# The largest |K| taken over blocks as they lie, then over 128 turned tokens, with a newly searched instruction order

## The chip, the cores and the metric

The kernel runs on one core of a Trainium2 chip. A core has five engines with a queue each: TensorE (PE; its weight loads are listed as PEld), VectorE (DVE), ScalarE (ACT), GpSimd (POOL) and SyncE (SP). TensorE writes its results to PSUM, here eight banks of 128 x 512 float32; VectorE and ScalarE read them there. The metric is the device time of one execution in microseconds (us).

## The reference

Two layers read inputs of 2048 tokens by 640 channels; their outputs stand side by side.

Part A is a gated long convolution. `k` is convolved with a filter of four taps and multiplied by `v`; the product `kv` is convolved over all 2048 tokens with a filter of its own per channel (by FFT in the reference), `kv * ssm_D` is added, and the sum is multiplied by `q`.

```python
y = irfft2(rfft2(kv_pad) * rfft2(kf_pad))[:, :S]
y = y + kv * ssm_D[None, None, :]
return q * y
```

Part B is attention with a memory: 32 heads of 20 channels, four segments of 512 tokens.

```python
logits = einsum('bhqd,bhkd->bhqk', qs, ks) * scale + mask
p = softmax(logits); a_dot = einsum('bhqk,bhkd->bhqd', p, vs)
pq = phi(qs); num = einsum('bhld,bhde->bhle', pq, M); den = einsum('bhld,bhd->bhl', pq, z) + 1e-06
o = g * (num / den) + (1.0 - g) * a_dot
M = M + einsum('bhld,bhle->bhde', phi(ks), vs); z = z + phi(ks).sum(l)
```

The heads are joined again and multiplied by `wo`.

## The kernel before

**The program is recorded, then issued in a stored order.** `Layer` calls `conv` for five blocks of 128 channels (`dp` 0 to 4) and `project` and `attend` for eight units `u` (segment `u // 2`, half `u % 2` of the heads), with `load_x` and `project_out` once a segment. None of these calls issues anything: a `Recorder` notes each instruction, or each run of matmuls under `rec.one()`, as an operation with its predecessors, and `price` (line 190) gives it a duration for an offline search. The result of that search stands in the file as two packed texts: `ORDER`, the place of every operation, and `BASE`, the first PSUM bank of every group of results. `issue` unpacks them and emits the operations in that order, so each engine's queue is the part of `ORDER` that belongs to it, and an instruction waits for those ahead of it on its engine and for the data it needs. All instructions have the line of `issue`, 253, in the profile; they are told apart by the tiles they write and read.

**Part A, per block.** `load_filter` brings 128 channels of `ssm_k` (tiles `ET` or `kT`) and turns them so that tokens lie on partitions: block 0 by TensorE matmuls with the identity `ident`, the others by a VectorE copy and a DMA transpose. `short_filter` applies the four taps (`kr`, `skd`) and multiplies by `vt`. `spectrum` multiplies by the DFT table `Wf`, copies eight PSUM results with ScalarE into `F` (one buffer, `FBUF = 1`, shared by both kinds and all blocks) and adds and subtracts on VectorE into `Xh` or `Kh` (keys `BX`, `BK`); in the first group of a filter's spectrum a matmul with weights `ones` adds `ssm_D` out of `Drow`, a 128 x 640 tile whose first row alone is not zero (line 459). `product` multiplies the spectra on VectorE (`pq`, `Y`), `inverse` goes back with `Wi`, multiplies by `q` (`outa`), and POOL's queue stores.

**Part B, per unit.** `project` (line 569) multiplies 128-token tiles of `xT` with `wqkv`. ScalarE copies K and Q into `KQ` (128 tokens, four tiles, K or Q, 16 heads, 32 places of which 20 are channels and the 21st of K is 1), and V into `Va`. SyncE's queue turns each tile by DMA into `KQT`, where head and channel lie on partitions and the tokens along them. `phi` makes `PP`, which is turned to `PqT`.

Softmax takes no row maximum. In its place a bound is subtracted inside the score's matmul: for each head and channel the largest |K| over the 512 tokens, `kam`, is taken on VectorE out of `KQT` (lines 607 and 608); `A` spreads it over the heads with a sign; |Q| (`qabs`, an AND with 0x7fff on `KQT`) is multiplied by `A` on TensorE; ScalarE copies the result to `bT`; and four small DMAs on SyncE's queue write its rows into `KQT`'s Q beside the ones of K. Every score of the unit needs them.

`attend` makes the scores block by block (A below the diagonal, D on it with the mask from `mleft` and `mright`, J for two joined), ScalarE takes the exponential of 128 x 1024 at a time into `ET` (seven buffers), TensorE multiplies by `Va` and adds the memory's part (`PqT`, `Mbd`), and VectorE divides (`rr`, `o`, `o_s`). `project_out` turns `o_s` and multiplies by `wo`.

**Constants.** POOL clears `Drow`, `ones`, the unused places of `KQ` and `PP`, and loads the small tables; SyncE and ScalarE load the weights.

Of the kernel before, what the change touches and what calls it, by code (L numbers as in the profile page):

```python
# [774 lines left out]
ORDER = r"""
c-jrrgLW7S5Cy>9yLan0we8flZKt+v+qP{dwQbwBZR@>nm~$qrq!5vG5?#_uJc%qRC6#25jFMUcC9_PI88TBKCNU8~;z~pb5S6b&2``x>jpUL@5?>NX42dbRB(@}!#FA7JNiwM<NhG<XMHO+0h1`-&
(jkjfm8=p?vP%LaL=MR*$&mtCkQLeRT`Ef=e3QgThB%TEv5^XCP)G_(5h*GKq@a|N(vnB=N(m_`#iY38ll)Rf%1U}<KxU*yAmShilA^Z6M;$3AHKmqRlOU-saS;z0kqI@Vu{4o}(pnlxC@C)$rGnI#
Hqu<`$~<W)4Wy~mlk8|Ap(Tv8k^&fjoM<LJkpsEV3%PL<c~B5-rJW2!d+8vZWE_U0qm0K0OhZ0&k<OAAQ6#F2L{}+<Q5cJ<7=*#-jXvlm6EF-DF&(2Z2K_Mwvt_R2M_H6dIdqr8=pnN(1HEJjW@0G5
qc7^A9~!`I5<=Nz{6G;D!v}oC94U%V_>2e^(duKCL^m_qLM%d0`H3I$3;z(#!dnzuEK6ke|Af7zugt*$%*8@kB&ARqWw2D1$$VKL^AT3mqFNsrD#N6oR6s>6MkTD2Xf_Y9^%BEY$p%?28)b!Tl7?uE
{!$zz@l!U-02wHQqy}oD7HXpoN+71Kl}4zHDu`uOQ4LKHgu1AXb+Sd8Vz@Lzh^&zjvRZ<rIliDR+MzvKpcVe2CB9*Z43@3Z0Y@dQZIkWN5u>CvcF0aSD7z%G?Unr!PTF9kbjBe$ES<1Vy5P8U#cnwu  # L780
-OwF><d+<gV{%eX$ZzR^J#t#A>sOqTB{(Bz<(x#a0Q-$UI4>9El7zM}wg&6a(pp(3>uj+tuB}BE>uPbVkzJI=*3Oz+Z|h@&t%3ElB$m`#STAd618lrZka!l~5?gyqXvwUDtwu*1XrpC}jFSX5S*Az`
f^iUsa9OU%dL**3vH?`rNixWW*kNphsOkz#lT}!Wzw%Fp8nm`9#WI-I)8sbHuF7&um20vCJFyG9F;Vs)j7HF~8c}b^b-5`~HJXOfy$G$hB%I!s=o(&QXk?9~QM8T*XkFch$8rFhuo+vh72EJcj$l6;
>QOY(V>pGTdKzc39p`WyZLPmGvpaGgXK(@CteM`Ei?}O~<RtpqLpgyAmeG3HWn95kTtj#3XRR%hwXy4HVwZ3O59GeY)LUq32{o3cwRD!=5^Hizp^3D<p0NhnSd-{&G|`vxN?yxOeIs!+jV9ID8du|K
GQESlNMR{$q&<~q@?2g>DtnA4c!)=MinN+iQ)y}q)O0%BnrnK^Y+3Cd?&AUC>j=wY88oB*vrL*<v+5`tZDVb`J+&<Q%!FfXoTauj)=~qlmA26D_QN`AC;e*QEHrCsHp^}~ET`qQT-ILmS$^xFd-RRH
wU3tDYG^Ipss*f|6|th0#|qg;`6OTDt-O<BmQ4#=cKsl2wVig>E}B4#TMjK@IrTN(;In+P+?q@CXjko~`Lv|9);9XtUfFB=W4raQm9=tK-ty}+yq6bviMM!%=Xh+Ttc;bmC-w>xtb$dxDpu91S&&sU
r}3RtvYJNLvf5V1s#{&FVfE~#g<^fnt6@0NK3G^zvI6?s!n2@8WCRw{!usCYuq~h43!7roY^qgZRerI#Hs6|Zo+-g*Y{&L&&K8_ywYW>?*iWm?aGY*+INN60UM-^g^p{0qHO{cbw!|h|ab0T5te6(n
07heEF1HmHg>@OkMqFSG`5q;-q%N}38kGyJjF#2zy53gVY74dy+hCh)jjgouT29y6M%!$MwTJf99d<;kXeq6#TdbG%)}6M?`sh{*((Sg*_Ui%d#%g*{cUw(1<{{l@`|W@ow7z=CqI0P3wLNy!y6~8_
W&<|iaa(7H?Su`}&K#^m^rQ{cL3+ea*+?CwUD=(dtrO2$3=Y>G9HFCijP}>DI!*`ZHjT&ljLDX4#ql~pdvT&xXAMr$$vQ>ru|E5-1NSolPwR2*&Fy+ZPwFYn&NEs;r|D6xs8e;i&d?k@t2x<EXX-4S
t#fsb9@F!7!Om+(UeL>WMX%X)J7?$gqFu7fcE#rDRl8w*8JqnWhjDp>H`$Z@dDCuLWxdAh9KetK#DpBgL`=;4+@TNnlmod`Z`&QaYxnHFC1Fxl(qz1-cNvTKcuAk|8B;MelQShB*h70{?-|H6Ov`jk
!4F)fulSmInUDFIff<>J3p6vcFg@pMR=(g%F4D!iL>KCJUe#+_fCX8I*Y$?p(!wmtBFx1+ys7uKxaVeBmScH7)(R}f;(VyzSb`P#KufX|pXeif%o6^NPxY?e(`<aMFSIo8=rb+prTn$N(L#QQh5ajQ  # L790
`E%Cx;Vi>S9Kj#_$&sw$w^-F*>MQ-lKfKM~9Lw<>$K|?0SLsR}%)cDPe>AWBf5k)iR!4I=#o_PtgO1@^U8mDHoijL-Ls{N8=xv?F6<o<-Ea$WNUO(!3oxn+4t)CgJA^J%x_(Xo;WKLlNujEr%**EGY
{j5v4S-0q1F6BJV=K?O|GS1;5e$lV`P1oou26HtFctH<g4PV2xe8aa~$Fg42H*ym<a|^d}F}HC8ziVh;&oExyf9MYG<SrKTu)dpn7|tX3cJAd*-N$-f+RJ!-Kfv%F*$=XzH}YTVAfk9wZ|X%nq6c^#
uj`S#sMAAvV}Hm;tmZ-Pp2U-S6F<VE{H+x|nn(8-9@AraGmq`byt%jX*51-nd7!8ExE{~r`yWl<Ej*zo_mm#T6Zv0F>?e7O$9aP3J%wlT%$~)wdN$AQIXr`B^faE<5AiU&`acz<^PHZ`b9)}o>-jvt
clS2l&5zL#3ZVhC^>#keNBL;K%qzS|#c5t*d+*@k5FQcG(K~r(@8UhYr$<CoL_>7MKyUBkeZ8Oe_W?f8m-`qGgO%RP2l-$h;zNCy5BC*5!pHhJAMa;4!6*7zUgad8?B}@5&oeBhcqB~q=|00}`YfOA
0hr@+eV$+T>psor`vPC+i+r)K@m0Rg*ZUG*>#O~gAN9z%;lUo_SNyau^@D!MkNFng>YIGCpYtd<?-#huxBCX)=!gBdpYS7o#xM9uzv;L9s_*cNzSH;kHNWj={gUtXeZI?g`+h&*{{i6J>gE
"""
# [76 lines left out]
```

## Time and profile before

| | |
|---|---|
| median of 3 runs | 290.04 us (289.86 to 291.36) |
| the profiled execution | 290.99 us, its span 289.2 us |
| TensorE's mean granted clock in it | 0.987 of full speed |
| VectorE busy | 262.0 us, 398 instructions |
| ScalarE busy | 254.0 us, 391 instructions |
| TensorE busy (matmuls; weight loads) | 258.5 us; 195.3 us, 4226 each |
| exponentials into `ET` | 155.9 us, 160 instructions |
| `kam` reductions on VectorE | 18.2 us, 8 instructions |

The span runs from the first instruction to the last; the execution's own time has 1.8 us more around it. Busy time is the time in which an engine's instructions run, counted once where they overlap. Matmuls are pipelined and their ends are modelled, so TensorE's busy time also holds time in which it could take more. Where a row gives an idle time, the name behind it is what ended it. Rows of the timeline give the start, the duration, the engine, the operation, what it writes and reads, and how many instructions were merged.

### The profile page before, as it was taken

To read this page: it belongs to the slowest core of one execution; us is meant where nothing else is said; L and a number is where in the kernel's file an instruction comes from. 1 tells how busy PE (TensorE), PEld (TensorE's weight loads), DVE (VectorE), ACT (ScalarE), POOL (GpSimd) and SP (SyncE) were. 2 spreads that over 40 slices of the span, in tenths; PEclk is the share of its full clock that TensorE was granted. 3 is DMA by queue.
4 is the path that set the end of the run, shared out by engine and by line. 5 is a ranking of instruction groups with operands and counts; after the bars stand their busy time and mean duration, and the time that the engine had idled before them with its cause. 6 is when DMAs were issued, how large, how long until landed. Compare 5 with 4: busy or idle time off the path is not lost. (4 is left out here: it accounts for less than half of the span.)

```text
span 289.2 us, 9883 instructions
## 1 busy us (share of the span) xinstructions
PE 258.5 (89%) x4226; PEld 195.3 (68%) x4226; DVE 262.0 (91%) x398; ACT 254.0 (88%) x391; POOL 42.5 (15%) x71
## 2 busy tenths in 40 slices
PE   0999998789989899999989999998799977888895
PEld 0788756668667678777656888656586755656673
DVE  0569999999999999999999999999999999989554
ACT  1694899899998978999999999999979999989972
POOL 8300000001005000403100310022001220001620
PEclk9999999999999989999999999999799999999999
DMA  6999889899943779916696149952492029921252
GB/s 190 383 243 178 217 160 174 207 215 164 223 118 85 165 99 204 205 61 120 166 167 144 43 59 174 191 133 71 88 156 57 24 55 141 207 26 48 58 123 91
DMA packets 113500, 40.71 MB, mean 141 GB/s; under 512 B 105696, under 2 KB 111376, under 8 KB 113328
## 3 DMA queue, kind: packets, MB, share of 16 engines
q1 hardware_dynamic: 108624, 34.07, 61.8%
q0 software_dynamic: 2064, 4.76, 5.5%
q10 hardware_dynamic: 2768, 1.24, 1.8%
q8 instruction: 33, 0.54, 0.8%
q14 instruction: 11, 0.09, 0.1%
HBM read 14.11 MB, written 5.24 MB: 67 GB/s over the span
## 5 line engine op out<-in xcount | busy, mean ns | idle before, releaser
L253 ACT ACTIVATE ET<-ps 128x1024 bf16<-128x1024 f32 x160 | 155.9, 1064 | 6.7 <-PE ps L253 6.4
L253 PEld LDWEIGHTS <-xT 128*128 128x128 bf16 x640 | 60.5, 99 | 32.2 <-issue 10.8
L253 PE MATMUL ps<-wqkv,xT 128*128 128x320 bf16 x480 | 75.5, 303 | 3.6 <-ACT ET L253 1.9
L253 ACT CAST F<-ps 128x512 bf16<-128x512 f32 x80 | 43.0, 614 | 4.2 <-DVE F L253 1.6
L253 POOL DMA_DIRECT2D out_dram<-outa x32 | 22.2, 815 | 165.1 <-DVE outa L253 141.1
L253 PEld LDWEIGHTS <-ET 128*128 128x128 bf16 x1296 | 40.3, 97 | 4.1 <-issue 2.2
L253 PE MATMUL ps<-Va,ET 128*128 128x21 bf16 x1280 | 41.2, 172 | 0.1
L253 PE MATMUL ps<-KQT 32*128 32x128 bf16 (+2 forms) x896 | 34.5, 242 | 2.0 <-ACT ET L253 1.0
L253 PEld LDWEIGHTS <-Wf 128*128 128x128 bf16 x320 | 29.9, 98 | 6.5 <-issue 2.4
L253 ACT CAST KQ<-ps 128x320 bf16<-128x320 f32 x64 | 27.5, 454 | 3.7 <-PE ps L253 3.1
L253 PE MATMUL ps<-wo,xT 128*128 128x320 bf16 x160 | 25.2, 299 | 1.1 <-ACT ET L253 0.6
L253 PEld LDWEIGHTS <-KQT 32*128 32x128 bf16 x896 | 16.5, 94 | 12.0 <-issue 10.8
L253 PE MATMUL ps<-skd,kr 128*128 128x128 bf16 (+3 forms) x140 | 20.9, 301 | 1.1 <-ACT ET L253 1.0
L253 PE MATMUL ps<-Y,Wi 128*128 128x256 bf16 x160 | 20.3, 273 | 1.7 <-ACT ET L253 1.0
L253 PE MATMUL ps<-vt,Wf 128*128 128x256 bf16 x160 | 20.1, 272 | 1.8 <-DVE vt L253 1.4
L253 PE MATMUL ps<-kT,Wf 128*128 128x256 bf16 x160 | 21.2, 276 | 0.0
L253 PEld LDWEIGHTS <-kr 128*128 128x128 bf16 x140 | 17.3, 146 | 5.5 <-issue 2.7
L253 DVE TENSOR_TENSOR o<-ps,rr 128x640 bf16<-128x640 f32 x24 | 19.7, 823 | 0.7
L253 PE MATMUL ps<-mright,mleft 32*128 32x128 bf16 x512 | 14.4, 219 | 6.5 <-ACT ET L253 3.4
L253 PE MATMUL ps<-Mbd,PqT 128*128 128x84 bf16 x96 | 18.2, 202 | 1.9 <-ACT ET L253 0.9
L253 DVE TENSOR_TENSOR Y<-Y,pq 128x2048 bf16<-128x2048 bf16 (+1 forms) x20 | 18.6, 949 | 0.1
L253 DVE TENSOR_TENSOR pq<-Xh,Kh 128x2048 bf16<-128x2048 bf16 x15 | 18.3, 1223 | 0.4
(77 smaller groups left out, 356.4 us busy)
## 6 DMA issues: line engine op xcount, KB each, us to landing
vt<-in_A_v_dram SPq DMA_DIRECT2D x10, 256.0 KB
pq<-in_A_q_dram SPq DMA_DIRECT2D x10, 256.0 KB
out_dram<-outa POOLq DMA_DIRECT2D x32, 64.0 KB, 2.5
out_dram<-outb POOLq DMA_DIRECT2D x12, 160.0 KB, 3.1
ET<-in_A_ssm_k_dram SPq DMA_DIRECT2D x3, 512.0 KB
Wf<-c_wf SPq DMA_DIRECT2D x2, 512.0 KB
Wi<-c_wi SPq DMA_DIRECT2D x1, 1024.0 KB
kT<-in_A_ssm_k_dram SPq DMA_DIRECT2D x2, 512.0 KB
```

What stands on the lines that cost most here:

```text
L253: f(*[fix(a) for a in args], **{k: fix(v) for k, v in kw.items()})
```

## The change

Three things change.

1. **The maximum.** Once a unit's four tiles of K lie in `KQ`, VectorE clears the sign bits of all 4 x 16 x 20 values (into the `qabs` buffer), takes the maximum of tiles 0 and 1 against 2 and 3, and of the two that are left, into a new tile `kmax`, 128 tokens by 16 heads by 32 places (places 20 to 31 are cleared once by POOL). Four matmuls with the identity turn `kmax`, 128 columns for four heads, into one PSUM bank, and `kam` is reduced out of that bank, 512 elements where it was 2048. The rest of the bound is as before.
2. **The D term.** `Drow` is 128 x 128 now, with the five blocks of `ssm_D` in its first five rows; the weights are column `dp` of the identity, repeated 128 times, instead of `ones`, which goes.
3. **The order.** `ORDER` and `BASE` are new: the search took a DMA transpose to last at least 1260 ns (line 205), and charged stretches in which TensorE has few columns to do. `order` and `base` differ throughout, on every queue. No line of code shows the charge.

```diff
@@ price
-                op.dur = 5.1 * size / 1024
+                op.dur = max(1260, 5.1 * size / 1024)
@@ Layer.__init__
-        self.Drow = c.tile([128, D], bf16, name="Drow")
-        self.ones = c.tile([128, 128], bf16, name="ones")
+
+        self.Drow = c.tile([128, 128], bf16, name="Drow")
+        self.kmax = c.tile([128, 16, 32], bf16, name="kmax")
         rec.key = ("zero",)
         nc.gpsimd.memset(self.Drow[:], 0.0)
-        nc.gpsimd.memset(self.ones[:], 1.0)
+        nc.gpsimd.memset(self.kmax[:, :, DH:32], 0.0)
         rec.key = ("load", "Drow")
-        nc.gpsimd.dma_start(out=self.Drow[0:1, :], in_=self.ssm_D[None, :])
+        nc.gpsimd.dma_start(out=self.Drow[0:5, :], in_=self.ssm_D.rearrange("(c d) -> c d", d=128))
@@ spectrum
                                 if last and h == 0:
-                                    nc.tensor.matmul(o[:, 0:128], lhsT=self.ones[:], rhs=self.Drow[:, dsl], start=False, stop=False, grp=g, skip_group_check=True)
+                                    nc.tensor.matmul(o[:, 0:128], lhsT=self.ident[:, dp:dp + 1].to_broadcast([128, 128]), rhs=self.Drow[:], start=False, stop=False, grp=g, skip_group_check=True)
@@ project
+        rec.key = ("kmax", u)
+        ka = self.ring("qabs", [128, 4, L])[:].rearrange("p g q -> p (g q)")[:, 0:1280].rearrange("p (t h d) -> p t h d", t=4, h=16)
+        V.tensor_scalar(out=ka.bitcast(i16), in0=KQ[:, :, 0, :, 0:DH].bitcast(i16), scalar1=0x7fff, scalar2=None, op0=ALU.bitwise_and)
+        V.tensor_tensor(out=ka[:, 0:2], in0=ka[:, 0:2], in1=ka[:, 2:4], op=ALU.max)
+        V.tensor_tensor(out=self.kmax[:, :, 0:DH], in0=ka[:, 0], in1=ka[:, 1], op=ALU.max)
+        g = self.group(1, "kmax")
+        with rec.one():
+            for k in range(4):
+                nc.tensor.matmul(g.ap[:, 0, 128 * k:128 * k + 128], lhsT=self.kmax[:, 4 * k:4 * k + 4, :], rhs=self.ident[:], start=True, stop=True, grp=g)
         rec.key = ("bound", u)
         kam = self.ring("kam", [128, 4], f32, n=2)
-        V.tensor_reduce(out=kam[:], in_=KQT[:, 0], axis=AX.X, op=ALU.max, apply_absolute_value=True)
+        V.tensor_reduce(out=kam[:], in_=g.ap[:, 0, :].rearrange("p (k t) -> p k t", k=4), axis=AX.X, op=ALU.max, grp=g)
@@ ORDER and BASE
...
```

More of the change, by code (lines that the diff above doesn't have):

```diff
@@ L775 @@
 ORDER = r"""
[L776 to L795, printed above, removed]
+c-jrrgMttW5Czb=cV=>JwrjI(+um&3wry{=YqM?Jwr#$5KH{X33=&z=N(6~6BB>=%(n&;#C+Q`#q>z;IRboj-fqa*5qCzoABMBtFM3o#8P2xy^#E^tCT`EZ;sUle<k|dU-l0=eATuCOmB)nu2mu!+%
@@ new lines @@
+vP)X#lypqMgpA2p%q__o$gIr5s*;V_nS(hQTcXGei7AyO1yeE+(=#zMu#gm%0#Z<lNpT4!u{l%Xu#}XR5>is~Nq))2+$<tRB@dG^kK~myQdZ(JBQr4#Ye;RWBk>p{)ug6Wm&~jsNmyQzG8N;qoTTPl
+sVEhsp)``bY%EQrzBHG*(m=vUJqazXrH!<dR`QTVSd_(BoGqlOG?TW{PWrMR^D#dQax}-VgS3~9GKrHpkcBveV>w3(a2zMHlMLff&f;)(l_?y>L7d6)tjNkN%&DBg{v5#0GMHUtwgk&8na1gyz}XCD
+C3X|)2#(|&c9$M9m%U^mdrAqGq$pIi6r*Z*jiAvqy2j8S5>X>*IhN-y{^mS})(V`@6<o<5{K@#bfQz`8%h+4`$`Z!WFxrTXxs(fJp{(K(2`ft_tj5(o(uBjL3afIFES74VCrvqDnlqjz&}Qr>bvRVQ
+>2lWPPpQZHY`}!tUk1oPStiS+G|RFK6YECVB<p0otdNzmN><AT36X|OqSaZ0L9EGI+$>upkq(j;Y{l9fEW>4ljFOfdB5P!=v}PN2WG8m!NNLN}+$&pUn{;7Uw&M;-s!_B91GGK&$##jYf7p#XWtZ%i
@@ new lines @@
+e>@-u<&bn|5B6j){$+1Q)=-*EcS~~pEq(Y)4$BewBQZ6W2I?L;E+^!u9Fx;>QqIUJIV<O+t9H}#V(QvP+v-pqrv0?PUXY8DLbq@m$IArS%68gbd+BHyBPq4FUXn?YO8aOy*~m1SPB(KC`)XR9EK}sN
+q}I+_16_2irq?l=L5J%A9iantyiSvGIzj)+Kgp=uxq}mRvQ8DlL~%^fOgdF}l2DxFX`Z5BJwrHFfZB+T7}&ro5)R>UfDsT8kr4$^5e@ZlRj$cF9^zph;SCulYq*Y+^eETzy4;jd2#rVxKp2F@ZK;D@
++|4~a#=1Dp6Wq&vyd_U$KO3SE&hQ)`%UNFHWj4iCUgI4(&raG?hv;?QU^Cp6n;fZE*j+F1Hb?6{xy6gjqj~iX@A9GC;~>qa_c=-%<Gu{m2YkdHnh-fPw?2{w5)-jd9}VzQUP)r)($_LglcIx8*Cx25
+Ne~B5<(VWxY{bQ5#zQi6)XbV3Sv8BkkyLobK%~KQdCe4f&Nobrba)|Y@q{VylrNYbGjyiT(%CvkYa$5oQ41N65ij|QZ@Cj4kzWhyTX`pYP(bHuu>R4%`c*R{6S5#HzG*g9`ygA9L$hlbqa{Fqg|f)j
@@ new lines @@
+94$~t3u_TAs>QUVhPBXETsz^tl+u<kYlYHUM$2jmEvFUqqkNJtk{#KQ136J%V_7a#(u!JHt7uitjXcPQul&Z({KD^i$M>wJA6P>_@)N6TUi{ME`dNasmWH#M8qwM!l6}^8sIB$1zBbT?`bDEz3~Qu6
+wXU|te66GNw5c}J<{H6ZZjH5tw$wIgqS39D#<cL3AF-{q{!_69S{%g?$KqN%Td46Zfpta~bVWBT)+PE~+aroC)gRgcQ7wseu#UD11yB&Zt&i=-8eOMrwYjyhgqFyPpePdCARBCj(bIa_N?oM`Y@n^y
+LTG30t);cHWx8CuqX$-KQcGqjExGN*KBTbq8fY7JlWx{-wnew<BHgANG(@{v36w->?AHT2%C>76ltoYM(4D$Vck3SAs|U3g`rwcr#t|IR-Z-o$bf2EoDmbdCtS`!=6#C(mRz)=&*JC=|_TvD~X?Gi8
+BkjDN)?s#5FX%-bZI^V6^|#B~*M_654aOP0s@L?o-q3M20$pqf`q@AX!WA8FH+6!I#u$vmL>q-$Iu_$F$;x3UhT*oRw!7LNlWhRDA){ro@knExth3$IDc0KB*bvKXL#?!xwFx+gL%42ZZ4xG8GRoK#
@@ new lines @@
+Oton?!)Dqnn{E|Q5tT6&(~#DtqleAFLw%&_EWN$f4E9F1<226TI8LAvPT~}1;ykKj2VUxBywWSUuMcz<W@8Q>YcQ5zE-nC0&u%&Ft%mWOwiIFggMIuzKJ#!M-oM)q%VJqAo8_`Rb{0o*41X=J<+J=&
+zzSM!`(yv?nHI8lb`H<=y%n*dR?Lc93A>0(sA!d~k`=a+_D<jHS9_vQ^_x|(YF6E9SXFz85Bfqs>L)E{zb(khTLqhsd02$SSb&ANifah)8@P^}_+q8(7Ve^fHMB-{4~^|Hp5Q(n;1z0GEvs#HtclgN
+&>q?ASrm`vpX{?m@;iv`^{uJh#&f*DQ#?ZxZ|d`GfwlJzKHtRadOdICjXj3P@rQVX*NExOESA5)5?gBByt}_eY@cn*@D9Ni)t6%>me~iaKwO_=y*-}4$49jCxwg<2Sp<*htFYG+c|vdL@jZdB##$`4
+by$xOY`{Ki?Q3nFt+x#pVjFD@mfL>&gpK%uP56v0*o+m{$5+}aTVq|ktFN}U-p+T~X4_(0ZJTYkJ+|BW`X<|9hwZ2xvD#k8zhb8yuy6Q*L*^dJk6A<ij{e@u586pPWvA_ob@mp1*3Q`pOXkPzf?c#r
@@ new lines @@
+_7j)wik-KscFmIe4ZCS6e1Ny{Ku_gAEv5JKU-)I|JcAGP^j_Z^ct`K#i9M;O_TNb2Lp`nc@Sbi=<AZ##5Alqi$uoNv&+6ISnceeyLH~nhUcifbF>mg7thnd!oSw^b`(4Z9dHpZ`VVDp15kAUC`e-lY
+g}t=jw+B|l%XxXP;AK3YSM*9=)+;+%#g!$zq~EfK_Q)RFZM$csTsYOIdsVOI)xCxXc}=h7(|nAN^-v7WFdXMAe3h?sFdV}(0>}FVe`&AmwY{;4KFO!}WPfJQEh?iiI%oJSpY1a}*ys3MpXc*^fgknN
+9+qo-p)c~qzQmXMGGFd*ZLP2K4Zhx=Scq@*r?$x>F@T%>sc-WwzTJ2DPT%FbeUBgW7q-<OdSo8=y}r-)`vE`bXZ(~$;aNZJNBo^1^27ewPxyO(<R|@^pY!wn-7onyzvGuZBJcWhf8k&Jx_|W_{@Abh
+RlndD{ipx(S000}{eyq>C;rmk_&5LUZ~c?s@SA?mZ~1+{?GOAv;JFDU
@@ L796 @@
 """
 BASE = r"""
-c-l=<0TRO?2#W~v{~r%R?7UtrB7_jE0XXn_vsQ;8%HCM?M0v7&S^L>p#c!S+o}I@7Ms@D4r;$)Gp@^V8p00sf7crc9MwDS=s?|&yHF(x6yH0Ws?gry9BUw2WW3-N#Z}ONm#jmTSSOx2Vh{m<m06m~(
-{C1_W?mAZ2UWyK343ANEGxHE<D{eFMb~-f{tzc%VtLc16<0QLaU(VhjT`#N4_s}-^OkSs+CdDt}7GH?d?e22EI=Ha#b?)MLgp``gDCyrMl70Vqy7JGXtAChBvq)*Uc(TMa^qrdpX*;h!{hN?o7&GHw
-tt3i{H;DLh`eWHMAOBQvRU9pyx<da-NK4n9_J@fH9gpYQn>RIeLzCE{=>tDfMh1%
+c-lpi2^In&3`0vd?tf#M-+<0@z%FSLFwLyZZL=<`vs-7^XBX!kmPGvQHt{@}b>3gk7ukw8y>>ERb&~looVCF(zNsm7Vntn3|5Y!l{nZR3XKl@NF<Mm4zCbBGVc#cEbXhy`Qf<Iz!+4);fPS-%>QOUV
@@ L801 @@
+?5y(+#SM-|Y_u)3ZIButuEwO#RXg4DYtTdf82g~d=tz*R&(5>KFDhMK4r+i|pbXcWb4@O3GQ0@!OtdumFSdzMyzZ6*gD|cJw`HoA&^D}Hr<l4K@p_ER-_ND`LG$NLK2J8M>hN^-8zoKdDmAgcF1H-~
+Py9Qz;rX4A;cUL!lh4uANt$B$W|(HXPWq~9kdl8*iD~MF*Q;^es>>_i>HFiE;x*IeE(SVVSj&Fy0tS!
 """
```

## The prediction

> **What bounds the kernel now.** I read the page first, then the span cut at three places, then the waits at those places. The first rows are the page's span, the busy time of each engine, and the 40 slices of the three compute engines and of TensorE's granted clock.
>
> ```profile
> span 289.2 us, 9883 instructions
> PE 258.5 (89%) x4226; PEld 195.3 (68%) x4226; DVE 262.0 (91%) x398; ACT 254.0 (88%) x391; POOL 42.5 (15%) x71
> ...
> DVE  0569999999999999999999999999999999989554
> ACT  1694899899998978999999999999979999989972
> ...
> PEclk9999999999999989999999999999799999999999
> ```
>
> Three engines look alike by share. The slices separate them: VectorE (DVE) is full from slice 3 to slice 35 and empty at both ends; ScalarE (ACT) has holes in the middle and is full just before the end. So the span is a relay. The busy time by stretch gives its legs (PE, PEld, DVE, ACT, POOL busy, clock, DMA share, GB/s):
>
> ```profile
> 0.00:21.20 21.20, 13.88 (x114) 11.10 (x114) 8.44 (x17) 12.46 (x25) 8.17 (x19) 1.00 0.95 273
> 21.20:211.20 190.00, 178.38 (x2747) 134.39 (x2745) 188.00 (x270) 173.09 (x275) 21.08 (x32) 0.98 0.76 147
> 211.20:279.50 68.30, 59.69 (x1287) 44.85 (x1284) 60.46 (x101) 65.93 (x84) 12.83 (x20) 1.00 0.50 86
> 279.50:289.20 9.70, 6.53 (x89) 4.93 (x86) 5.15 (x13) 2.53 (x9) 0.47 (x1) 0.96 0.33 103
> ```
>
> Leg one is the fill: VectorE does 8.44 us of work in 21.20 and idles 12.76. Leg two is VectorE's: 188.00 busy of 190.00, while ScalarE idles 17. Leg three is ScalarE's: 65.93 of 68.30. Leg four is the last attention block's values, the output projection and its store. The hand-over between legs two and three is in the timeline: `F` has one buffer, so ScalarE can copy the last filter block's spectrum into it only after VectorE has read the input's.
>
> ```profile
> 209.96 1.23 DVE L253 TENSOR_TENSOR F<-F 128x2048 bf16<-128x2048 bf16 x1
> 212.42 1.29 DVE L253 TENSOR_TENSOR Xh<-F 128x1024 bf16<-128x1024 bf16 x2
> 211.27 1.56 ACT L253 CAST F<-ps 128x512 bf16<-128x512 f32 x3 [1.09 <-DVE F L253]
> 213.74 1.56 ACT L253 CAST F<-ps 128x512 bf16<-128x512 f32 x3 [0.57 <-PE ps L253]
> ```
>
> Two reads of F (F<-F, then Xh<-F, done at 213.71) each release some copies. From there ScalarE's queue runs almost full to the last exponential.
>
> **The maximum: what it costs on VectorE.** Per attention unit (eight of them) the 2048-element reduction goes, and four instructions come: an AND over 1280 elements, a maximum over 640, one over 320, and a reduction of 512 elements from PSUM. The rows give the old one and the nearest shapes of the new ones, each followed by the row that starts after it without a wait.
>
> ```profile
> 29.12 2.28 DVE L253 TENSOR_REDUCE kam<-KQT 128x4 f32<-128x2048 bf16 x1
> 31.32 0.68 DVE L253 TENSOR_SCALAR qabs<-KQT 128x2048 int16<-128x2048 int16 x1
> ...
> 37.45 0.49 DVE L253 TENSOR_SCALAR qabs<-KQ 128x1280 bf16<-128x1280 bf16 x1
> 37.86 1.29 DVE L253 TENSOR_TENSOR Xh<-Xh 128x1024 bf16<-128x1024 bf16 x2
> ...
> 244.55 0.48 DVE L253 TENSOR_TENSOR PP<-PP,qabs 128x640 bf16<-128x640 bf16 x1
> 244.95 1.22 DVE L253 TENSOR_TENSOR Y<-Y,pq 128x2048 bf16<-128x2048 bf16 x1
> ...
> 256.50 0.32 DVE L253 TENSOR_TENSOR o_s<-o 128x320 bf16<-128x320 bf16 x1
> 256.74 0.48 DVE L253 CAST outb<-ps 128x320 bf16<-128x320 f32 x1
> ...
> 264.49 0.69 DVE L253 TENSOR_TENSOR vt<-ps,pq 128x512 bf16<-128x512 f32 x1
> 265.09 0.68 DVE L253 TENSOR_TENSOR Y<-Xh 128x1024 bf16<-128x1024 bf16 x1
> ```
>
> A full engine pays from start to start: 2.20 us goes, 0.41 + 0.40 + 0.24 + 0.60 = 1.65 comes, and I add 0.03 for a reduction against a product of that size: 1.68, a saving of 0.52 us per unit, 4.2 for eight. By durations instead, 2.28 against 0.49 + 0.48 + 0.32 + 0.69 = 1.98, it is 0.30. I take 0.52, since the engine is full, and keep 0.30 as the other end.
>
> The Trainium skill speaks against the split here (VectorE: DVE Perf Modes, the section on the TRN2 errata): every instruction with its source in SBUF pays a fixed time, which it measures at about 150 cycles, so many small ones pay it many times. An estimate from that page is (2048 + 150) - (320 + 320 + 160 + 512 + 4 x 150) = 286 cycles, 0.30 us per unit, as the durations have it; six units would then give 1.8 us where I count 3.1, and the time would be 288.9. The trace disagrees in part: the starts lie about 0.08 us closer than the durations.
>
> **What of it shortens the span.** Only work ahead of the hand-over counts; later VectorE has slack (60.46 of 68.30). In the new kernel's list, units 0 to 5 have their maximum ahead of the Xh<-F read and units 6 and 7 after it: 6 x 0.52 = 3.1 us less. Other VectorE instructions ahead of it differ by under 0.1. On ScalarE's side the new list has two copies fewer (an F and a KQ) ahead of the first copy that needs this read; their 0.9 us is left over for leg three. So 3.1 - 0.9 = 2.2 us is gained there. At the earlier hand-over (F<-F) the gain is 3.3; both must be met, so the smaller counts.
>
> **TensorE, POOL, SyncE.** TensorE gets 32 matmuls of 128 columns. The 16 turning matmuls on the filter are the same shape.
>
> ```profile
> 10.83 0.65 PEld L253 LDWEIGHTS <-ET 128*128 128x128 bf16 x4
> 11.10 0.63 PE L253 MATMUL ps<-ident,ET 128*128 128x128 bf16 x4
> 12.37 0.66 PE L253 MATMUL ps<-ident,ET 128*128 128x128 bf16 x8
> ```
>
> Eight in 0.66 us spans some 0.06 to 0.08 each: 0.3 us per unit, 2.4 in all, off the path while TensorE leads. Where the lead is short it is a wait: in units 5 and 6 only 0.76 and 0.87 us of VectorE work stands between writing `kmax` and reducing its turned copy; the four matmuls and two hand-overs need some 0.7 if TensorE is free. I add 0.2 us for these two. The D term keeps its ten matmuls and loads; its weights are now an identity column repeated. At zero; were repeated columns to load at twice 98 ns, ten loads make 1.0 us, on TensorE. POOL's memsets change by fractions of a us and stand before its first use of them. The reduction no longer waits for the four transposes of K, but the AND over `KQT` still does, and on SyncE nothing is removed. The changed price of a transpose only steered the search: the order is stored.
>
> **The fill.** The order differs most visibly here.
>
> ```profile
> 9.76 1.54 PE L253 MATMUL ps<-wqkv,xT 128*128 128x320 bf16 x5
> ...
> 16.51 2.02 PE L253 MATMUL ps<-kT,Wf 128*128 128x256 bf16 x17
> 17.14 4.01 ACT L253 CAST F<-ps 128x512 bf16<-128x512 f32 x8
> 21.19 1.23 DVE L253 TENSOR_TENSOR Kh<-F 128x2048 bf16<-128x2048 bf16 x1 [1.73 <-ACT F L253]
> ```
>
> Before, the first projection runs at 9.76 while the filter lands; now the four turns come first. The filter was there by 10.83 at the latest, so TensorE starts this block 0 to 1.1 us later, and one more KQ copy (0.4) stands among the eight F copies: Kh<-F starts at 21.6 to 22.7. But by then VectorE has done 10.2 us of work instead of 8.4: the first unit's maximum fills the 1.73 us wait. Its idle is 11.4 to 12.5 instead of 12.76: 0.3 to 1.4 gained, of which a later wait for the X spectrum, behind the same chain, may take back up to 1. I take 0.4, between 0 and 1.1.
>
> **The sum.** 2.2 + 0.4 - 0.2 = 2.4 us off the profiled span: 286.8. That execution took 290.99 us, 1.8 around the span, and the median of the three runs is 290.04. I lay the difference on the median: **287.6 us**. With the saving at 0.30 per unit it is 288.9, with the fill's best 286.9.
>
> **Rivals.** (1) Slower: TensorE's queue stops at `kmax`. The four matmuls wait for VectorE's last maximum, and behind them stand scores that ScalarE needs. For it: such waits exist. Against it: they are few.
>
> ```profile
> PE ps L253 <- DVE o L253: 2.3, 4, 0.8
> DVE rr L253 <- PE ps L253: 3.5, 5, 1.3
> ```
>
> At the longest, 0.8 us for each of eight units is 6.4, less my 2.4: 294.0. It decides from 0.3 us per unit on.
> (2) No visible change: leg two's balance. ScalarE was already 91% busy there (173.09 of 190), and TensorE more; a VectorE that is 3.1 us quicker finds them late and idles instead. Lost is the 2.2, kept 0.2: 289.8.
> (3) More: the charge on stretches of few columns works. Around the second clock dip the trace shows (203 to 206, 206 to 210, then the chain of waits):
>
> ```profile
> 203.00:206.00 3.00, 1.78 (x45) 0.95 (x43) 3.00 (x5) 2.53 (x5) 0.00 (x0) 1.00 0.39 89
> 206.00:210.00 4.00, 3.80 (x65) 2.78 (x65) 3.97 (x8) 4.00 (x5) 0.00 (x0) 0.57 0.52 70
> ...
> 206.20 10.80 PE ps L253 x178
> ```
>
> A stretch with TensorE 1.78 us busy of 3 is followed by a mean clock of 0.57 over 4 us, and the chain runs through TensorE just then. Without the dip, (1 - 0.57) x 4 = 1.7 us of it goes: 287.6 - 1.7 = 285.9. The Trainium skill has the rule (TensorE: Matmul & The Clock Gate, Part 1): after an idle window of about 3.4 us the clock falls to half, and after a busy one it returns. The trace agrees in length, though TensorE was thinly busy there, not idle. Against it: the dip is one of two, and the other (slice 15) is on no chain that I see.
>
> **How the numbers follow.** Chances: the forecast 0.52, rival 1 0.18, rival 2 0.20, rival 3 0.10. The forecast's own range is 286.2 to 289.0. The range to give reaches 284.5 below (rival 3 with the fill's best) and 292.0 above, which takes in rival 2 and rival 1 up to 0.55 us per unit. What this kernel's runs can tell from no change is about 0.5%, 1.45 us: faster is below 288.6, slower above 291.5. Faster: most of the forecast (0.45) and rival 3 (0.10): 0.55. Within: the rest of the forecast and most of rival 2: 0.26. Slower: 0.19.
>
> **What would show it.** Right: VectorE's busy time near 258; the four new groups at 1.9 to 2.0 us of durations per unit; VectorE idle 12 to 13 us before the middle; the last filter block's Xh<-F done near 211; ScalarE's exponentials ending near 277. Wrong: TensorE waits released by `kmax`, VectorE waits before `kam` over 0.3 us, or a middle in which VectorE idles 5 us instead of 2, each points to its rival; a clock below 0.987 to the third one's reverse.

## The result, and the profile after

The changed kernel takes 288.88 us, the median of 11 runs (287.95 to 289.5); the kernel before took 291.22 us in 11 runs beside them (289.86 to 293.25). The ratio is 0.9918, 95% interval 0.9898 to 0.9938: 2.4 us less (1.8 to 3.0). The profiled execution of the changed kernel took 288.88 us, with a span of 287.1 us.

The page's first parts for the changed kernel: the span, the busy times, and the slices of VectorE, ScalarE and TensorE's granted clock.

```profile
span 287.1 us, 9970 instructions
PE 258.5 (90%) x4258; PEld 195.5 (68%) x4258; DVE 259.5 (90%) x422; ACT 253.8 (88%) x391; POOL 42.3 (15%) x71
...
DVE  0679899999999999999999999999999999998653
ACT  1593799999899998999989999998999999999962
...
PEclk9999999999999999999999999999999999999998
```

VectorE lost 2.5 us of work and has 24 instructions more. Both clock dips of before (slices 15 and 29) are gone. The legs of the relay are read again from the busy time by stretch, now cut at the hand-over itself (the end of the last `Xh<-F` that frees `F` for the last filter block) and at the end of the last exponential. First before, then after (columns: PE, PEld, DVE, ACT, POOL busy, clock, DMA share, GB/s).

```profile
0.00:213.71 213.71, 194.77 (x2909) 147.84 (x2910) 198.91 (x290) 187.44 (x303) 29.25 (x51) 0.98 0.79 160
213.71:279.53 65.82, 57.21 (x1233) 42.52 (x1232) 58.01 (x98) 64.06 (x80) 12.86 (x20) 1.00 0.48 82
279.53:289.20 9.67, 6.50 (x88) 4.90 (x86) 5.12 (x13) 2.50 (x8) 0.44 (x1) 0.95 0.33 103
```

```profile
0.00:21.20 21.20, 13.28 (x111) 11.11 (x112) 9.86 (x19) 12.02 (x25) 7.74 (x19) 1.00 0.98 284
0.00:211.42 211.42, 192.73 (x2928) 147.67 (x2929) 197.05 (x308) 186.65 (x302) 29.02 (x51) 1.00 0.80 161
211.42:276.93 65.51, 59.18 (x1246) 42.86 (x1245) 57.11 (x102) 64.59 (x81) 12.59 (x20) 1.00 0.49 89
276.93:287.10 10.17, 6.62 (x87) 4.92 (x85) 5.32 (x14) 2.57 (x8) 0.65 (x1) 0.93 0.27 87
```

The hand-over comes 2.29 us earlier (213.71 to 211.42). What stands behind it is almost as long as it was: 65.51 against 65.82 to the last exponential, 10.17 against 9.67 for the tail. Ahead of it VectorE is 1.86 us less busy (198.91 to 197.05) and idles 0.43 us less (14.80 to 14.37). So most of the time left where it was meant to leave: 1.86 + 0.43 + 0.31 - 0.50 = 2.1 us of span. The timeline of the changed kernel at the hand-over:

```profile
209.89 0.69 DVE L253 TENSOR_TENSOR Xh<-F 128x1024 bf16<-128x1024 bf16 x1
210.73 0.68 DVE L253 TENSOR_TENSOR Xh<-F 128x1024 bf16<-128x1024 bf16 x1
...
211.50 0.58 ACT L253 CAST F<-ps 128x512 bf16<-128x512 f32 x1 [0.21 <-DVE Xh L253]
```

ScalarE's wait for `Xh` is now 0.21 us; its copy starts 0.09 us after VectorE's read ends at 211.41. The groups of the new maximum, from the changed kernel's lines kept apart by shape (busy time, mean ns, then the idle time before them and what ended it):

```profile
L253 DVE TENSOR_REDUCE kam<-ps 128x4 f32<-128x512 f32 x8 | 5.5, 683 | 0.0
L253 DVE TENSOR_SCALAR qabs<-KQ 128x1280 int16<-128x1280 int16 x8 | 3.9, 490 | 0.2
L253 DVE TENSOR_TENSOR qabs<-qabs 128x640 bf16<-128x640 bf16 x8 | 3.9, 485 | 0.0
L253 DVE TENSOR_TENSOR kmax<-qabs 128x320 bf16<-128x320 bf16 x8 | 2.5, 312 | 0.1
L253 PEld LDWEIGHTS <-kmax 128*128 128x128 bf16 x32 | 2.1, 98 | 1.1 <-DVE kmax L253 1.0
```

Four instructions of 0.68 + 0.49 + 0.49 + 0.31 = 1.97 us stand in place of one of 2.28: 0.31 us per unit by durations. TensorE waits for `kmax` 1.0 us in all, and VectorE never for the turned copy.

In the queue the price is another, since an instruction that waits for nothing starts some 0.08 us before the one ahead of it ends. The AND and the two maxima of one unit stand in the changed kernel's timeline like this:

```profile
87.93 0.48 DVE L253 TENSOR_TENSOR PP<-PP,qabs 128x640 bf16<-128x640 bf16 x1
88.44 0.49 DVE L253 TENSOR_SCALAR qabs<-KQ 128x1280 int16<-128x1280 int16 x1
88.85 0.68 DVE L253 TENSOR_TENSOR vt<-ps,vt 128x512 bf16<-128x512 f32 x1
89.45 0.48 DVE L253 TENSOR_TENSOR qabs<-qabs 128x640 bf16<-128x640 bf16 x1
89.85 0.34 DVE L253 TENSOR_TENSOR Mbd<-Mbd,o 128x336 bf16<-128x336 bf16 x1
90.11 0.32 DVE L253 TENSOR_TENSOR kmax<-qabs 128x320 bf16<-128x320 bf16 x1
90.34 1.28 DVE L253 TENSOR_TENSOR vt<-ps,vt 128x512 bf16<-128x512 f32 x2
```

Counted over the traces, each instruction from its start to the next start (or to its own end, if that comes first), the six old reductions ahead of the hand-over take 13.18 us, 2.20 each. The 24 new instructions take 10.25, 1.71 per unit: 2.93 us less, 0.49 per unit. But the other 283 VectorE instructions there, the same in both kernels but for one of 0.32 us, take 186.72 us where they took 185.65: 1.07 more, 0.27 of it in longer durations and the rest in overlap that the new order loses. At 88.44, and so in four of the six units, the AND writes the buffer `qabs` that the instruction ahead of it reads, and starts only behind its end. The busy time keeps 2.93 - 1.07 = 1.86. That 6 x 0.31 gives the same figure is a coincidence.

### The profile page after: what moved, and what is told of

Its sections match the earlier page's. It is cut to its first block, busy times and chain, and to the rows that moved or that the text cites. A ratio compares the mean times of both kernels' runs of the same rounds, so it can differ in the third digit from the quotient of the medians.

```text
span 287.1 us, 9970 instructions
## 1 busy us (share of the span) xinstructions
PE 258.5 (90%) x4258; PEld 195.5 (68%) x4258; DVE 259.5 (90%) x422; ACT 253.8 (88%) x391; POOL 42.3 (15%) x71
## 5 line engine op out<-in xcount | busy, mean ns | idle before, releaser
L253 PEld LDWEIGHTS <-xT 128*128 128x128 bf16 x640 | 59.6, 98 | 29.4 <-issue 7.4
L253 PE MATMUL ps<-wqkv,xT 128*128 128x320 bf16 x480 | 74.0, 300 | 1.9 <-ACT ET L253 1.9
L253 ACT CAST F<-ps 128x512 bf16<-128x512 f32 x80 | 44.1, 626 | 2.3 <-PE ps L253 1.0
L253 PE MATMUL ps<-KQT 32*128 32x128 bf16 (+2 forms) x896 | 33.8, 239 | 2.5 <-DVE o L253 1.2
L253 ACT CAST KQ<-ps 128x320 bf16<-128x320 f32 x64 | 26.9, 467 | 4.2 <-PE ps L253 3.1
L253 PE MATMUL ps<-wo,xT 128*128 128x320 bf16 x160 | 25.9, 299 | 0.8 <-ACT ET L253 0.5
L253 PE MATMUL ps<-vt,Wf 128*128 128x256 bf16 x160 | 20.9, 272 | 1.1 <-ACT F L253 0.5
L253 PE MATMUL ps<-skd,kr 128*128 128x128 bf16 (+3 forms) x140 | 20.3, 292 | 0.9 <-DVE o_s L253 0.4
```

What stands on the lines that cost most here:

```text
L253: f(*[fix(a) for a in args], **{k: fix(v) for k, v in kw.items()})
```

## The experiments

Ratios are to the kernel before, run on the same chip; a difference to the changed kernel is the ratio less 0.9918, times 291.2 us, with an uncertainty of 0.9 to 1.4 us by the intervals.

| run | ratio (95%) | median, us |
|---|---|---|
| `e_newmax_oldorder` | 1.1244 (1.1195 to 1.1294) | 328.06 |
| `e_newmax_units0to5` | 1.0511 (1.0479 to 1.0542) | 306.6 |
| `e_oldmax_neworder` | 1.0379 (1.0345 to 1.0412) | 302.26 |
| `e_oldmax_neworder2` | 1.0545 (1.0504 to 1.0586) | 306.94 |
| `e_drow_alone` | 1.0002 (0.9978 to 1.0026) | 291.51 |
| `e_short_reduce` | 0.9925 (0.9895 to 0.9954) | 288.9 |
| `e_no_and_units0to5` | 0.9920 (0.9889 to 0.9952) | 288.4 |
| `e_pad_units0to5` | 1.0152 (1.0120 to 1.0183) | 296.05 |
| `e_pad_units6and7` | 1.0222 (1.0186 to 1.0258) | 298.04 |
| `e_pad_spread_ahead` | 1.0118 (1.0075 to 1.0162) | 293.6 |
| `e_pad_spread_behind` | 1.0049 (1.0025 to 1.0072) | 292.41 |
| `e_pool_add` | 1.0014 (0.9992 to 1.0036) | 291.61 |

### The maximum in the old order, the old reduction in the new one

Theory 1 is the prediction's: VectorE's work ahead of the hand-over sets the end. Theory 2: the new order brings the gain. First each part was set into the other's order by hand.

```diff
# before.py, ORDER: the old list, the kmax instructions set in near kam
+        rec.key = ("kmax", u)   # AND, two maxima, four turning matmuls
-        V.tensor_reduce(out=kam[:], in_=KQT[:, 0], ...)
+        V.tensor_reduce(out=kam[:], in_=g.ap[:, 0, :]..., grp=g)
```

> The kernel before with the new maximum (and the smaller D term, which makes room for its tile), in the old order: the new instructions are set in by hand near the old reduction, the rest of the list stays. Theory 1 (VectorE's work ahead of the hand-over sets the end): six units at 0.45 us, as the new trace has them from start to start, are 2.7 us less ahead of the hand-over; some of it may go to waits of the hand-set turns, so -1.5 to -2.7 us, a ratio of 0.991 to 0.995, and VectorE's busy time about 2.5 us lower. Theory 2 (the new order, with its clock, brings the gain, and the maximum only makes room): no change, 0.998 to 1.002.

It took 36 us more than the kernel before. The waits of this kernel (us in all, times, longest) name the main reason:

```profile
PEld L253 <- DVE kmax L253: 25.5, 7, 6.8
```

TensorE's queue reached the turns up to 6.8 us before VectorE had the maximum, and everything behind them stood. This is the first rival's mechanism, at full size. The second try set the turns by the start times that the trace of before shows, and left units 6 and 7 alone.

> The kernel before, old order, with the new maximum in units 0 to 5 only (and the smaller D term, for the space). Each turn now stands in TensorE's queue behind matmuls that began, in the trace of before, at least 0.3 us after the third maximum could be done, so that the queue need not stop there; the reduction moves up. The earlier try lost 25 us to TensorE stopped at the turns. Theory 1 (VectorE's work ahead of the hand-over): 6 x 0.45 = 2.7 us less there, -1.5 to -2.7 us, a ratio of 0.991 to 0.995; TensorE's waits released by the maxima under 2 us in all. Theory 2 (the order brings the gain): 0.998 to 1.002. Theory 3 (in an order that was not searched with it the turn costs more than it saves, however it is set in): above 1.005, with TensorE's waits for the maxima above 5 us.

```profile
ACT KQ L253 <- DVE qabs L253: 8.3, 2, 6.6
DVE kam L253 <- PE ps L253: 8.1, 2, 6.2
PEld L253 <- DVE kmax L253: 0.2, 1, 0.2
```

TensorE no longer stops at the turns (0.2 us), but VectorE now waits for two of them, 8.1 us, since they stand behind other matmuls; and ScalarE may not write the next unit's K into `KQ` before the AND has read it (8.3 us). Theory 3 has the number, with another wait than it named: 15 us more.

```diff
# after.py, its order; no kmax instructions
-        V.tensor_reduce(out=kam[:], in_=g.ap[:, 0, :]..., grp=g)
+        V.tensor_reduce(out=kam[:], in_=KQT[:, 0], axis=AX.X, op=ALU.max, apply_absolute_value=True)
```

> The changed kernel with the old reduction over the turned K, at the places that the new order gives to the reduction or just behind the AND; no turn of the maximum. Theory 1: VectorE is as busy as before, about 262 us, and the time is back at that before within 0.3% (0.997 to 1.003), though the clock dips may stay away. Theory 2: the gain stays, a ratio of 0.990 to 0.994. A clock near 0.997 beside a time as before would show that the dips cost nothing.

> The changed kernel with the old reduction, now at the places that the new order gives to the reduction out of PSUM (in unit 0 ahead of the AND); in the earlier try it stood behind the AND, and TensorE waited 11 to 14 us for the product A. VectorE's work is that of before. Theory 1: the 2.7 us come back, a ratio of 0.998 to 1.004 to the kernel before. Theory 2: 0.990 to 0.994, as the changed kernel. A clock at 0.99 or more with the time of before would show that the clock does not matter here.

Both are slower than either kernel. In the first, TensorE waits for the product `A`; in the second, where the reduction stands early, VectorE waits for the transposes of K and passes it on. The waits of the one, then of the other:

```profile
PEld L253 <- DVE A L253: 13.7, 7, 3.0
```

```profile
DVE kam L253 <- DMA KQT<-KQ: 8.6, 2, 5.1
```

These four settle nothing between the theories. They show that neither maximum could be set by hand into the other's order without loss: a wait of a few us in one place of these queues costs more than the whole change brings.

### The D term, and the clock

```diff
# before.py, old order
-        nc.tensor.matmul(o[:, 0:128], lhsT=self.ones[:], rhs=self.Drow[:, dsl], ...)
+        nc.tensor.matmul(o[:, 0:128], lhsT=self.ident[:, dp:dp + 1].to_broadcast([128, 128]), rhs=self.Drow[:], ...)
```

> The kernel before with the D term's new form alone (weights are one column of the identity, repeated). Both theories: no change, within 0.2% of the time before; the ten weight loads stay at 98 ns and the ten matmuls at 219 ns. If repeated columns loaded slower, the loads would show it.

No change. Its span, its clock in slices, and its rows by shape:

```profile
span 290.2 us, 9882 instructions
...
PEclk9999999999999999999999999999999999999999
```

```profile
L253 PE MATMUL ps<-Drow,ident 128*128 128x128 bf16 x10 | 2.2, 219 | 0.0
L253 PEld LDWEIGHTS <-ident 128*128 128x128 bf16 x10 | 1.0, 98 | 0.2
```

Loads and matmuls cost what they did. The profiled execution had no clock dip at all and still a span 1.0 us longer than the one of before with its two dips. That alone does not clear the clock: 0.85 us of it was lost in the fill, where the first `Kh<-F` started at 22.04 us in place of 21.19, and from there to the last exponential this execution was 0.69 us quicker (257.65 against 258.34). The runs point the same way. In this kernel those with a mean clock of 0.998 or more took 291.0 us on average (3 runs), those with 0.990 or less 292.4 (5); in `e_short_reduce`, below, 288.4 (7) and 289.4 (4); in the kernel before beside these two, 291.6 (5) and 291.7 (6) on the one chip, 290.4 (8) and 291.5 (2) on the other. The clock of the kernel before averaged 0.994 in its 57 runs of this section, that of the changed kernel 0.998, about two fifths of the step between those groups. By an estimate from these figures the steadier clock is worth up to some 0.5 us of the 2.4: a part of the gain, not the gain.

### The same saving with nothing moved

```diff
# before.py, old order
-        V.tensor_reduce(out=kam[:], in_=KQT[:, 0], ...)
+        V.tensor_reduce(out=kam[:], in_=KQT[:, 0, :, 0:432], ...)
```

> The kernel before, old order, nothing moved: each reduction of K takes 432 of the unit's 512 tokens per channel (it leaves out 80 tokens of the bound), 1728 elements in place of 2048. By the old row (2.28 us for 2048) that is some 0.33 us less per unit, about what the new maximum saves by VectorE's busy time (1.86 us for six units), with no turn and no new wait. Theory 1 (VectorE's work ahead of the hand-over sets the end): -1.5 to -2.2 us, a ratio of 0.992 to 0.995. Theory 2 (only the new order brings the gain): 0.998 to 1.002.

The group by shape, the first `Kh<-F`, and the stretches to the hand-over (at 211.92) and from there to the last exponential:

```profile
L253 DVE TENSOR_REDUCE kam<-KQT 128x4 f32<-128x1728 bf16 x8 | 15.6, 1946 | 0.0
```

```profile
20.52 1.22 DVE L253 TENSOR_TENSOR Kh<-F 128x2048 bf16<-128x2048 bf16 x1 [1.35 <-ACT F L253]
```

```profile
0.00:211.92 211.92, 194.02 (x2910) 147.31 (x2910) 197.30 (x290) 186.97 (x304) 29.17 (x51) 0.98 0.79 162
211.92:277.69 65.77, 57.16 (x1233) 42.47 (x1231) 57.34 (x97) 64.04 (x80) 12.82 (x20) 1.00 0.47 81
```

0.33 us per unit off VectorE (2279 to 1946 ns), with the old order and the old waits, moves the hand-over 1.79 us (1.61 of it VectorE's busy time, 198.91 to 197.30) and the time by a ratio of 0.9925. The whole change has 0.9918. One execution is a rough witness here: 0.67 of the 1.79 us is there at 20.52, ahead of the first reduction (21.19 before), so that 1.12 comes behind the fill. The 12 runs against 23 carry the reading: 2.2 us less (1.3 to 3.1), at the same mean clock of 0.995. Theory 1 holds, and theory 2 falls: a saving on VectorE of this size, in the old order, is enough to explain the gain. What is left for the order, 0.2 us, has an uncertainty of 1.0.

### More work, ahead of the hand-over and behind it

```diff
# after.py: e_pad_units0to5 has n = 2 in units 0 to 5, e_pad_units6and7 n = 6 in units 6 and 7
+        for n in range(...):
+            V.tensor_scalar(out=ka.bitcast(i16), in0=KQ[:, :, 0, :, 0:DH].bitcast(i16), scalar1=0x7fff, ...)
# e_pad_spread_ahead, e_pad_spread_behind: twelve of them one at a time, kr onto itself
+    V.tensor_scalar(out=kr[:, 16:1296].bitcast(i16), in0=kr[:, 16:1296].bitcast(i16), scalar1=0x7fff, ...)
```

> The changed kernel with the AND over 1280 elements done three times in place of once in units 0 to 5 (the same values written again): 12 more instructions at 0.43 us, 5.2 us of VectorE, all ahead of the hand-over. Theory 1 (work ahead of the hand-over counts one for one): 4.2 to 5.7 us more than the changed kernel, a ratio to before of 1.006 to 1.012. Rival (leg two is balanced, TensorE and ScalarE would have been late anyway): under 3 us, below 1.002. Rival (TensorE stops at the turns, which now come late): more than 6 us, above 1.013.

> The changed kernel with the AND done seven times in place of once in units 6 and 7: the same 12 instructions and 5.2 us of VectorE, but behind the hand-over, where it had 8.4 us of idle time in 66. Theory 1: 0 to 1.5 us more than the changed kernel, a ratio to before of 0.991 to 0.997. Rival (VectorE's work counts alike wherever it stands): 4 to 6 us more, 1.005 to 1.012.

> The changed kernel with twelve more ANDs over 1280 elements on VectorE (on the tile kr, which nothing reads any more), one at a time among the instructions that start between 184 and 208 us: not in the chain of a unit's maximum, ahead of the hand-over. They add 12 x 0.49 = 5.9 us of VectorE. Theory 1: 5 to 6.5 us more than the changed kernel, a ratio to before of 1.009 to 1.014.

> The same twelve ANDs, one at a time every 5 us between 215 and 270 us, behind the hand-over and in no unit's maximum. The earlier six in a row in units 6 and 7 cost more than their length, since all that waits for those maxima came late. Theory 1, corrected (behind the hand-over VectorE has room for single instructions, 8.4 us of idle time in 66, and not for a lump ahead of a unit's scores): 0 to 2 us more than the changed kernel, 0.991 to 0.999. Rival (there is no room behind the hand-over either, VectorE's work counts one for one to the end): 5 to 6.5 us more, 1.009 to 1.014.

Ahead of the hand-over twelve more ANDs cost 5.8 us spread and 6.8 us in the maximum's chain (4.3 and 7.1 in the profiled spans). VectorE's busy time ahead of it grows by 4.38 us (197.05 to 201.43) and 6.15 (to 203.20), and the hand-over moves by 4.03 and 6.83. The spread ones are the clean test: they take 4.84 us from start to start, 0.40 each where the duration is 0.49, and count about one for one, as theory 1 had it. In the chain the ANDs write the same buffer one after the other and do not overlap (0.49 each), and TensorE's weight loads wait 4.2 us for `kmax` where they waited 1.0: the result lies above theory 1's range, where the rival with TensorE's turns had put it, so the two causes are mixed there. The stretch behind the hand-over keeps its length, 65.86 us in both. First the spread ones, then those in units 0 to 5:

```profile
0.00:215.45 215.45, 193.62 (x2929) 147.51 (x2930) 201.43 (x320) 186.73 (x302) 29.35 (x51) 0.99 0.76 158
215.45:281.31 65.86, 59.12 (x1246) 42.81 (x1244) 57.11 (x102) 64.61 (x81) 12.58 (x20) 1.00 0.47 88
```

```profile
0.00:218.25 218.25, 194.21 (x2926) 147.64 (x2929) 203.20 (x320) 187.48 (x302) 29.09 (x51) 0.99 0.76 156
218.25:284.11 65.86, 59.17 (x1246) 42.86 (x1245) 57.11 (x103) 64.60 (x81) 12.60 (x20) 1.00 0.48 88
```

Behind the hand-over theory 1 fails. Six in a row in units 6 and 7 cost 8.9 us, more than the 6 us or so that they take. Spread out, twelve cost 3.8. In that second kernel the last unit's product `A` and the last exponentials tell where they count; the rows are `A` in the changed kernel and in the spread one (durations in ns, then first and last start).

```profile
L253 DVE TENSOR_TENSOR A<-sel,kam x1: 291/291/291, 247.3 to 247.3; 128x128 bf16<-128x128 bf16 x1
```

```profile
L253 DVE TENSOR_TENSOR A<-sel,kam x1: 291/291/291, 250.8 to 250.8; 128x128 bf16<-128x128 bf16 x1
```

Of the twelve, the last ahead of it starts at 248.66 and the first behind it at 253.61. The stretch from the hand-over to the last exponential, of the spread kernel:

```profile
210.82:280.35 69.53, 61.34 (x1246) 43.73 (x1245) 61.47 (x115) 65.17 (x81) 12.77 (x20) 0.98 0.42 83
```

Seven of the twelve stand ahead of unit 7's `A`, which comes 3.5 us later though the hand-over was 0.6 earlier: 4.1 us for 7 x 0.49 = 3.4 of work. The five behind it cost nothing: from `A` to the last exponential it is 29.6 us in both (247.3 to 276.93, 250.8 to 280.35). So VectorE's queue counts until the last unit's bound is made, not only until `F` is handed over. The busy time of the changed kernel behind the hand-over, cut once more, shows why:

```profile
211.00:250.00 39.00, 35.30 (x662) 24.81 (x661) 38.41 (x68) 38.46 (x54) 5.53 (x8) 1.00 0.61 98
250.00:270.00 20.00, 18.16 (x450) 13.73 (x449) 15.77 (x29) 19.49 (x22) 4.37 (x7) 1.00 0.27 62
```

VectorE idles 0.59 us of the 39 up to 250 us, as little as ScalarE (0.54); its room begins there. For the lump of six, the trace of that kernel from 205 us on has TensorE waiting for VectorE's division in `o`, which frees the bank (6.2 us, 0.8 in the changed kernel), and ScalarE's exponentials waiting for TensorE:

```profile
PE ps L253 <- DVE o L253: 6.2, 4, 2.7
ACT ET L253 <- PE ps L253: 6.0, 6, 2.6
```

### Still less work on VectorE

```diff
# after.py, units 0 to 5
-        V.tensor_scalar(out=ka.bitcast(i16), ...)      # the AND
-        V.tensor_tensor(out=ka[:, 0:2], in0=ka[:, 0:2], in1=ka[:, 2:4], op=ALU.max)
+        V.tensor_tensor(out=ka[:, 0:2], in0=KQ[:, 0:2, 0, :, 0:DH], in1=KQ[:, 2:4, 0, :, 0:DH], op=ALU.max)
```

> The changed kernel without the AND over 1280 elements in units 0 to 5 (the first maximum reads K as it lies in KQ, so the maximum is of signed values there: the absolute value is left out). VectorE has six instructions less, 0.43 us from start to start, 2.6 us, all ahead of the hand-over. Theory 1: still VectorE's leg, 2.0 to 2.9 us less than the changed kernel, a ratio to before of 0.981 to 0.986. Rival (the other engines are now as late as VectorE): under 1 us less, 0.988 to 0.992.

The rival's number came: a ratio of 0.9920, no gain over the changed kernel that the runs can tell (0.1 us more, with an uncertainty of 1.1), where theory 1 had at least 2.0.

```profile
0.00:211.03 211.03, 193.14 (x2928) 148.12 (x2929) 195.03 (x302) 186.37 (x302) 29.01 (x51) 1.00 0.78 161
211.03:276.53 65.50, 59.20 (x1246) 42.87 (x1245) 57.11 (x103) 64.59 (x81) 12.58 (x20) 1.00 0.48 88
```

VectorE is 2.02 us less busy ahead of the hand-over (197.05 to 195.03) and idles 1.63 us more (14.37 to 16.00), so 0.39 is left. Of that idle time 1.00 lies ahead of the first `Kh<-F`, which waits for ScalarE's copies into `F` and starts at 22.74 where it started at 22.32; unit 0's maximum stands in that fill. The other 0.63 lies in small places behind it, where 0.81 us was gained. What sets the pace there, and how much of the fill is chance of one execution, is open.

The other way to relieve VectorE was to give work to GpSimd:

```diff
# after.py, units 2 to 4: the last addition of each head group
-                V.tensor_tensor(out=odst, in0=o2[:, 0]..., in1=o2[:, 1]..., op=ALU.add)
+                nc.gpsimd.tensor_tensor(out=odst, in0=o2[:, 0]..., in1=o2[:, 1]..., op=ALU.add)
```

> The changed kernel with the last addition of each head group of units 2 to 4 (o2 plus o2 into o_s, 320 elements, 12 of them) on GpSimd in place of VectorE. Theory 1: ten of them stand ahead of the hand-over, at 0.24 us from start to start: VectorE has 2.4 us less there, and the time falls by up to 2.4 us against the changed kernel, a ratio to before of 0.984 to 0.990, unless VectorE then waits for GpSimd at the single buffer o2. Theory 2 (VectorE no longer sets the end once the order is balanced): as the changed kernel, 0.990 to 0.994. A rival of its own: GpSimd's additions slow VectorE's instructions beside them, and the time rises above the changed kernel's.

The rival of its own holds, 2.8 us more than the changed kernel. Its timeline shows what happens beside an addition on GpSimd:

```profile
214.62 0.96 POOL L253 TENSOR_TENSOR o_s<-o 128x320 bf16<-128x320 bf16 x1 [6.40 <-DVE o L253]
214.97 0.96 DVE L253 TENSOR_SCALAR qabs<-KQ 128x1280 int16<-128x1280 int16 x1
...
217.59 0.68 DVE L253 TENSOR_TENSOR Xh<-Xh 128x1024 bf16<-128x1024 bf16 x1
217.75 1.17 POOL L253 TENSOR_TENSOR o_s<-o 128x320 bf16<-128x320 bf16 x1 [2.17 <-DVE o L253]
218.18 0.91 DVE L253 TENSOR_TENSOR kmax<-qabs 128x320 bf16<-128x320 bf16 x1
```

No version was found that beats the changed kernel.

## Why the prediction was right, and where it was not

**The time.** Forecast: 2.4 us off, 287.6 us. Measured: 2.4 us off (1.8 to 3.0), 288.88 us. The difference between the two is the base: the forecast stood on the median of three runs, 290.04, and eleven runs gave 291.22.

**The relay and its hand-over** stand. The forecast had the end of `Xh<-F` near 211 and the last exponential near 277; they came at 211.42 and 276.93. The stretch between them is 65.50 to 65.86 us in six kernels (before, after, shorter reduction, no AND, both pads ahead), while the hand-over moves over 7 us.

**The size of the maximum's saving** was nearly right: 0.52 us per unit forecast from start to start, 0.49 measured. By durations it is 0.31, and the estimate from the Trainium skill (VectorE: DVE Perf Modes, the section on the TRN2 errata), 0.30, agrees with the durations.

**"Other VectorE instructions ahead of it differ by under 0.1" was wrong**: these 283 instructions took 1.07 us more in the new order, so that 1.86 us of busy time was left of the 2.93. For the same reason VectorE's busy time came to 259.5 us in place of "near 258": over all eight units the maximum saves 3.9, and the others take 1.3 more. Where the starts stand, and which instructions lose their overlap, was not asked of the new list. In one order the loss is smaller: where the reduction was shortened the others took 0.4 us more for 2.0 saved, without the ANDs 0.5 more for 2.5, while two executions of unchanged instructions differ by 0.2 to 0.3.

**Why the sum still came out** is luck in part: two mistakes nearly cancelled. The forecast charged 0.9 us for ScalarE's copies that are left over for the stretch behind the hand-over. ScalarE did get 0.53 us more work there (64.06 to 64.59), but it idled 0.84 less (1.76 to 0.92), and the stretch got 0.31 shorter. So 3.1 - 0.9 = 2.2 was forecast from these terms, and 2.93 - 1.07 + 0.31 = 2.17 came.

**The fill** was right. The idle time ahead of 21.2 us fell from 12.76 to 11.34, a gain of 1.42, and later waits of the second leg took back 0.99 (2.04 to 3.03), 0.74 of it in one wait for ScalarE's copy of the input's spectrum at 31.71: 0.43 net ahead of the hand-over, 0.4 forecast. In three kernels of the old order the first `Kh<-F` starts at 20.52, 21.19 and 22.04 us in one execution each, so that so close a hit is luck too.

**TensorE's turns and the D term** were about right: 1.0 us of waits for `kmax` in all, none of VectorE for `kam`, where the forecast charged 0.2 us; the D term at zero was measured alone.

**"Only work ahead of the hand-over counts" was wrong**: up to unit 7's `A`, 36 us later, single instructions count one for one or more (4.1 us for seven of 0.49), and a lump ahead of a unit's scores counts more. The slack of 60.46 in 68.30 us was read as room; in the changed kernel it begins behind that `A`.

**The rivals.** The first (TensorE stops at `kmax`) needed 2.4 us of waits and had 1.0, but in an order that was not made for it the same wait was 25.5. The second (balance) did not decide here: 2.0 us saved in the old order came through in the runs. At the next step 2.0 us more gave 0.39 at the hand-over and nothing in the time that the runs can tell. The third (clock) saw its dips vanish, and the runs give that up to some 0.5 us, not 1.7. Its lower bound was mis-added: with the fill's best it is 286.9 - 1.7 = 285.2, not 284.5.

## What to carry to other kernels

Find the point up to which the full engine's work sets the end, and test it with idle instructions put ahead of it and behind it; here the stretch after the hand-over stayed constant, and the point lay later than the trace suggested. Price several short instructions for a long one from start to start, but do not hold the rest of a newly ordered queue constant: its overlaps change too. Shorten the long one alone as a control: it shows what the saving is worth without the new order. A replacement that adds a trip through another engine's queue must be placed with the whole order, since turns set in by hand cost six to fifteen times what the change brings (14.9 and 36.2 us against 2.4). Ask what the next saving meets, because here 2.0 us more of it brought nothing that the runs can tell. And compare many runs before one trace with another, since the fill alone moved by more than half of the change.

## What the runs showed of the hardware

GpSimd and VectorE stand in each other's way. An addition of 320 bf16 elements takes 0.32 us on VectorE and 0.78 to 1.70 on GpSimd (mean 1.01, 12 of them). Where it began first, a VectorE instruction that reads SBUF alone grew by most of the overlap: the AND 0.49 to 0.96 us, the 320-element maximum 0.32 to 0.91; `rr<-ps` (0.35) and `outa<-ps,pq` (0.68), which read PSUM, kept their time; over all instructions that overlapped, 3.4 us in sum, more than the 12 x 0.24 = 2.9 that VectorE was spared; it also waited 2.0 us for GpSimd. Where VectorE's `Xh<-Xh` had begun first it kept its 0.68, and GpSimd's addition took 1.17. The Trainium skill has this rule (SBUF — State Buffer, the section "Who interferes with whom"): the two share a pair of ports under an exclusive lock, and the later one is blocked. The trace agrees.

TensorE's granted clock is not a property of the order: the runs of the kernel before had means from 0.986 to 1.000. In the kernels `e_drow_alone` and `e_short_reduce` the runs at 0.998 or more were 1.4 and 1.0 us shorter than those at 0.990 or less.

VectorE's instructions overlap: an AND of 0.49 us among others costs 0.40 to 0.42 us of the queue, and 0.49 or more where it writes the buffer that the one ahead of it wrote.
